# Contiguous head loads cast by DMA, head pairs in the halves of the PE array, and a sorting matrix spread by PE, in a block-sorted attention with an FFN behind it

## Chip, cores, metric

One core of a Trainium2 chip. The metric is device time in microseconds (us). "Span" is the time from the first to the last instruction in the trace; the timed run is about 2 us longer. A ratio is the mean time of one kernel's fast runs over the mean of the fast runs of the kernel before in the same rounds, so not quite the ratio of the medians that are quoted. Engines are PE (TensorE matmul), PEld (its weight loads), DVE (VectorE), ACT (ScalarE), POOL (GpSimd), SP (SyncE). "Granted clock" is the share of its full clock that PE was given; "eviction" is the copy of a product out of PSUM, where PE writes, into SBUF. In the lines of the profile scp are the scores, et their exponentials, vbp and vs the transposed v, oup the attention output, xtp its transpose, tp (before: ktp, vtp) the mixed k or v, qtp the transposed q, and hp and op the two products of the FFN.

## The reference, cut to what matters

```python
# q, k, v: (4 batches, 8 heads, 768 tokens, 64), sort_net: (4, 8, 8, 8); block = 96 tokens
P = sort_net
for _ in range(5):                       # exp, then divide by row sums and column sums
    ...
k_sorted = einsum('bhij,bhjcd->bhicd', P, k_blocks)     # mix the 8 blocks of k, and of v
v_sorted = ...
attn = softmax(scale * q_blocks @ k_sorted_blocks^T)    # 96 x 96 in each block
x = (attn @ v_sorted_blocks)  ->  (3072 tokens, 512)
out = relu(x @ w_in)**2 @ w_out                          # the FFN: 512 -> 2048 -> 512
```

There are 32 heads, which the changed kernel takes as 16 pairs, and 768 FFN matmuls of 128 x 128 by 512.

## The kernel before

What the change and the argument touch; `# ...` marks cuts.

```python
# sorting matrix: through DRAM, then spread to 128 partitions
nc.sync.dma_start(out=pt_dram.transpose([1, 0, 2]), in_=p_tr)
for j in range(NB):
    nc.sync.dma_start(out=ptall[16 * j:16 * j + 16, :, :],
                      in_=pt_dram[j].partition_broadcast(16))
w_all[...] = mask * ptall                      # DVE, per batch
# ...
for b in range(B):
    for h in range(H):                         # one head at a time
        # q as one load, k and v in 16-row pieces; q and k cast to bf16 on ACT
        for c in range(NC):
            nc.sync.dma_start(out=kf[:, c, :], in_=k_r[hd, :, 16 * c:16 * c + 16, :])
            nc.gpsimd.dma_start(out=vb[:, c, :], in_=v_r[hd, :, 16 * c:16 * c + 16, :])
        nc.scalar.copy(out=qb, in_=qf)
        nc.scalar.copy(out=kb, in_=kf)
        # ... transposes of q; k and v mixed by w_all; permuted on eviction
        for i in range(NB):
            nc.tensor.matmul(out=scp[:, i, 0:BLK], lhsT=ksT[:, i, :],
                             rhs=qT[:, BLK * i:BLK * (i + 1)], start=True, stop=True)
        nc.scalar.activation(out=et, in_=scp[:, :, 0:BLK], func=AF.Exp, scale=scale)
        # ... vs from vsT; then attn @ v with et as weights, divide, transpose to xT
for mc in range(MC):                           # FFN: matmuls, relu on ACT, square on DVE
    # ...
```

The softmax here doesn't subtract the row's maximum and nothing guards it: scores larger than these inputs give would overflow.

## Time and profile before

| | kernel before |
|---|---|
| median of 3 runs | 338.93 us (338.56 to 339.76) |
| span | 336.6 us |
| granted PE clock, mean | 0.954 |
| PE busy | 287.8 us (86%) |
| ACT busy | 130.2 us (39%) |
| exponentials | 32, 0.807 us each |

Two more lines of the page: the chain of waits that ended last, as shares of the span by engine, and the group of the exponentials (busy time, mean ns of one, idle time of ACT before them and what ended it).

```profile
PE 82%; SPq 6%; DVE 4%; DMA 4%; issue 1%; POOL 1%; ACT 1%; ACTq 0%; DVEq 0%
```

```profile
L198 ACT ACTIVATE et<-scp 96x768 bf16<-96x768 f32 x32 | 25.8, 807 | 38.6 <-PE scp L192 38.1
```

One exponential covers 768 columns in 807 ns.

### The profile page before, as it was taken

Reading aid. Unit: us, or ns where it says so; the run is one execution under the profiler, and the core shown is the slowest. Engines: PE = TensorE matmul, PEld = TensorE weight load, DVE = VectorE, ACT = ScalarE, POOL = GpSimd, SP = SyncE. Lnnn points to the kernel's source line nnn. Section 1 sums busy time; section 2 is a strip of 40 time slices with the busy share of each in tenths; the row PEclk is TensorE's granted clock in tenths of the full one; section 3 lists DMA queues with packets and bytes.
Section 4 is the critical chain, followed back from the end, with each engine's and each line's share of the span. In section 5 each row is a group of like instructions: output and inputs, shape, how many; then the busy total and the mean of one; then the engine's idle time right before and its main releaser. Section 6 shows DMA issues by size and latency. Waiting matters only on the chain.

```text
span 336.6 us, 6099 instructions
## 1 busy us (share of the span) xinstructions
PE 287.8 (86%) x2240; PEld 159.5 (47%) x2240; DVE 171.9 (51%) x338; ACT 130.2 (39%) x222; POOL 130.1 (39%) x267
## 2 busy tenths in 40 slices
PE   1012576776999999999999999999999999999995
PEld 0011455555555555555555555555544444444442
DVE  3443455655678655667765567776634204303400
ACT  3210322323455524365543255641136316425611
POOL 9483687447445564464455644650000000000000
PEclk9999995756799999999999999999999999999999
DMA  5579999857455575765556764321010010011011
GB/s 87 92 105 208 185 158 173 122 91 82 65 65 83 68 116 94 119 107 69 72 82 101 113 129 60 17 16 37 34 64 0 31 64 31 0 62 66 0 62 62
DMA packets 110366, 26.87 MB, mean 80 GB/s; under 512 B 104576, under 2 KB 106752, under 8 KB 110336
## 3 DMA queue, kind: packets, MB, share of 16 engines
q0 software_dynamic: 55104, 7.45, 26.2%
q1 hardware_dynamic: 55232, 19.03, 22.6%
q8 instruction: 17, 0.28, 0.3%
q14 instruction: 13, 0.11, 0.1%
HBM read 27.40 MB, written 6.30 MB: 100 GB/s over the span
## 4 chain that ended last, share of the span: by engine, by line
PE 82%; SPq 6%; DVE 4%; DMA 4%; issue 1%; POOL 1%; ACT 1%; ACTq 0%; DVEq 0%
PE hp L245 27%; PE op L257 26%; PE ktp L170 5%; PE oup L213 5%; PE vbp L203 5%; PE scp L192 4%; SPq L146 4%; PE qtp L161 4%; PE vtp L181 4%; DMA kf<-in_k_dram 4%; PE xtp L230 2%; DVE ao L222 2%; SPq L101 1%; DVE ksT L174 1%; DVE vs L208 1%
## 5 line engine op out<-in xcount | busy, mean ns | idle before, releaser
L150 POOL DMA_DIRECT2D vb<-in_v_dram x192 | 114.3, 626 | 85.6 <-PE vtp L181 76.1
L245 PE MATMUL hp<-xT,w_in_bf 128*128 128x512 bf16 x384 | 97.5, 385 | 0.0
L257 PE MATMUL op<-w_out_bf,h 128*128 128x512 bf16 x384 | 94.4, 380 | 0.0
L251 ACT ACTIVATE h<-hp 128x512 bf16<-128x512 f32 x96 | 57.2, 596 | 30.6 <-PE hp L245 30.5
L252 DVE TENSOR_TENSOR h<-h 128x512 bf16<-128x512 bf16 x96 | 40.0, 421 | 55.8 <-ACT h L251 55.5
L245 PEld LDWEIGHTS <-w_in_bf 128*128 128x128 bf16 x384 | 33.5, 98 | 36.2 <-issue 1.4
L257 PEld LDWEIGHTS <-h 128*128 128x128 bf16 x384 | 33.3, 98 | 35.6
L198 ACT ACTIVATE et<-scp 96x768 bf16<-96x768 f32 x32 | 25.8, 807 | 38.6 <-PE scp L192 38.1
L156 ACT CAST qb<-qf 128x384 bf16<-128x384 f32 x32 | 16.4, 512 | 52.4 <-PE qtp L161 50.4
L170 PE MATMUL ktp<-w_all,kb 128*64 128x128 bf16 x192 | 19.4, 247 | 19.3 <-DVE w_all L109 17.4
L174 DVE CAST ksT<-ktp 64x768 bf16<-64x768 f32 x32 | 30.3, 948 | 10.1 <-PE ktp L170 9.6
L263 ACT COPY ob<-op 128x512 f32<-128x512 f32 x24 | 14.0, 584 | 44.0 <-PE op L257 44.0
L185 DVE CAST vsT<-vtp 64x768 bf16<-64x768 f32 x32 | 30.1, 940 | 1.5 <-PE vtp L181 1.5
L157 ACT CAST kb<-kf 128x384 bf16<-128x384 f32 x32 | 16.4, 511 | 34.0 <-DMA kf<-in_k_dram 24.5
L208 DVE COPY vs<-vbp 96x512 bf16<-96x512 bf16 x32 | 13.5, 421 | 31.0 <-PE vbp L203 31.0
L170 PEld LDWEIGHTS <-kb 128*64 128x64 bf16 x192 | 14.3, 125 | 29.9 <-issue 21.6
L213 PE MATMUL oup<-vs,et 96*96 96x65 bf16 x256 | 18.1, 218 | 12.2 <-ACT et L198 7.7
L213 PEld LDWEIGHTS <-et 96*96 96x96 bf16 x256 | 15.3, 134 | 22.2 <-ACT et L198 13.0
L192 PEld LDWEIGHTS <-ksT 64*96 64x96 bf16 x256 | 15.2, 131 | 17.1 <-DVE ksT L174 12.8
L192 PE MATMUL scp<-qT,ksT 64*96 64x96 bf16 x256 | 19.3, 221 | 4.4 <-DVE ksT L174 4.4
L161 PE MATMUL qtp<-ident,qb 128*64 128x128 bf16 x192 | 18.7, 240 | 4.4 <-POOL mask L62 4.4
L222 DVE TENSOR_TENSOR ao<-oup,rec 96x512 bf16<-96x512 f32 x32 | 21.8, 683 | 0.7
(31 smaller groups left out, 168.3 us busy)
## 6 DMA issues: line engine op xcount, KB each, us to landing
qf<-in_q_dram SPq DMA_DIRECT2D x32, 192.0 KB
kf<-in_k_dram SPq DMA_DIRECT2D x192, 32.0 KB
out_dram<-ob SPq DMA_DIRECT2D x24, 256.0 KB
vb<-in_v_dram POOLq DMA_DIRECT2D x192, 16.0 KB, 2.3
w_in_bf<-in_moe_w_in_dram POOLq DMA_DIRECT2D x4, 512.0 KB, 8.7
w_out_bf<-in_moe_w_out_dram POOLq DMA_DIRECT2D x16, 128.0 KB, 4.8
ptall<-pt_scratch SPq DMA_DIRECT2D x8, 16.0 KB
p_sb<-in_sort_net_dram SPq DMA_DIRECT2D x1, 8.0 KB
```

Source lines behind the costliest of these rows:

```text
L150: nc.gpsimd.dma_start(out=vb[:, c, :], in_=v_r[hd, :, 16 * c:16 * c + 16, :],)
L161: nc.tensor.transpose(out=qtp[:, 128 * c:128 * (c + 1)], in_=qb[:, c, :], identity=ident)
L170: nc.tensor.matmul(out=ktp[:, 128 * c:128 * (c + 1)], lhsT=kb[:, c, :], rhs=wh, start=True, stop=True)
L174: nc.vector.tensor_copy(out=ksT.rearrange("p i (a c) -> p i a c", c=CH).transpose([0, 2, 1, 3]), in_=ktp.rearrange("p (a b c) -> p a b c", ...
L185: nc.vector.tensor_copy(out=vsT.rearrange("p i (a c) -> p i a c", c=CH).transpose([0, 2, 1, 3]), in_=vtp.rearrange("p (a b c) -> p a b c", ...
L192: nc.tensor.matmul(out=scp[:, i, 0:BLK], lhsT=ksT[:, i, :], rhs=qT[:, BLK * i:BLK * (i + 1)], start=True, stop=True)
L213: nc.tensor.matmul(out=oup[:, i, 0:D + 1], lhsT=et[:, i, :], rhs=vs[0:96, i, 0:D + 1], start=True, stop=True)
L222: nc.vector.tensor_tensor(out=ao2[:, :, h % 2, :], in0=oup[:, :, 0:D], in1=rec[:, :, None].to_broadcast([96, NB, D]), op=ALU.mult)
L245: nc.tensor.matmul(out=hp, lhsT=w_in_bf[:, kc, 128 * nt:128 * (nt + 1)], rhs=xT[:, kc, 512 * mc:512 * (mc + 1)], start=(kc == 0), stop=(kc ...
L251: nc.scalar.activation(out=h1, in_=hp, func=AF.Relu)
L252: nc.vector.tensor_tensor(out=h2[:, nt, :], in0=h1, in1=h1, op=ALU.mult)
L257: nc.tensor.matmul(out=op, lhsT=h2[:, nt, 128 * mt:128 * (mt + 1)], rhs=w_out_bf[:, nt, :], start=(nt == 0), stop=(nt == NT - 1))
```

## The change

Its intent: fewer and larger loads (a row is 6 tokens x 64 of one head, contiguous, and DMA casts), two heads at once in the halves of the PE array, full 128-column weights so that they load fast, and no trip through DRAM for the sorting matrix. Since a partition now holds the six consecutive tokens 6p to 6p+5, tokens come out of the products in another order: by a (0 to 5) first, then by c (0 to 15 in a block). They must be put back somewhere. For q nothing is done (the query order within a block is free until the output); for k and v the eviction reads PSUM permuted; for the exponential the write is permuted. The core of the diff:

```diff
-        kf, vb: 6 loads each per head (16 rows x 64); kb, qb cast by nc.scalar.copy
+    q_r = q.rearrange("b h (p a) d -> b p h (a d)", a=NA)          # NA = 6, likewise k, v
+    nc.gpsimd.dma_start(out=t[:, n * g:n * (g + 1), :], in_=src[b, :, n * g:n * (g + 1), :])
-    pt_dram store, eight broadcasts, w_all = mask * ptall
+    pt = ps1.tile([128, NB, NH], FP32, tag="p1")
+    for i in range(NB):
+        nc.tensor.matmul(out=pt[:, i, :], lhsT=pb[:, i, :, :]..., rhs=ident[0:NH, 0:NH], ...)
+    w_all = mask * pt
+    for a in range(NA):                       # q, k, v: both heads by turns, column halves
+        for e in range(2):
+            nc.tensor.matmul(out=tp[64 * e:64 * (e + 1), a, :], lhsT=src[:, hA + e, ...], rhs=w[e], ...)
+            nc.gpsimd.memset(sT[:, S:S + 32], 0.0)      # pads, behind the loads in GpSimd's queue
+        for hf in range(2):                   # scores: both heads by turns, row halves
+            scp = ps2.tile([128, 2, 512], FP32, tag="p2")
+            ...
-            nc.scalar.activation(out=et, in_=scp[:, :, 0:BLK], func=AF.Exp, scale=scale)
+            for e in range(2):
+                nc.scalar.activation(
+                    out=et[:, e, 384 * hf:384 * (hf + 1)].rearrange(
+                        "p (n c a) -> p n a c", c=C0, a=NA),
+                    in_=scp[0:96, e, 0:384].rearrange("p (n a c) -> p n a c", c=C0, a=NA),
+                    func=AF.Exp, scale=scale)
+                    # output: 128 columns of et as weights, 32 of them beyond the block
+                    lhsT=et[:, e, BLK * i:BLK * i + 128],
... FFN as before, but called between the pairs, with three PSUM buffers for both halves
```

## The prediction

> **What bounds the kernel now.** I read the 40 slices first, then a table of five stretches, then single stretches in order of time, then the waits.
>
> The slices split the run in three: PE is hardly busy up to slice 3, is patchy under a lowered clock in slices 5 to 10, and is full from there to the end.
>
> ```profile
> PE   1012576776999999999999999999999999999995
> PEclk9999995756799999999999999999999999999999
> ```
>
> The stretches, in us from the start of the span (columns: length; busy time and count of PE, PEld, DVE, ACT, POOL; granted clock; DMA share; GB/s):
>
> ```profile
> 0.00:37.00 37.00, 4.71 (x42) 4.06 (x42) 13.70 (x38) 7.12 (x15) 24.44 (x59) 1.00 0.80 126
> 37.00:86.00 49.00, 36.52 (x341) 28.54 (x341) 28.73 (x48) 12.81 (x21) 30.96 (x60) 0.71 0.91 130
> 86.00:110.00 24.00, 24.00 (x207) 12.82 (x204) 18.10 (x35) 14.43 (x25) 12.26 (x24) 0.94 0.53 73
> 144.00:250.00 106.00, 106.00 (x961) 57.98 (x960) 69.92 (x132) 46.11 (x79) 44.71 (x91) 1.00 0.46 69
> ```
>
> Start (0 to 37): 42 matmuls. Slow stage (37 to 86): about seven heads of attention, chains of dependent steps. Dense stage (86 to the end): PE never waits, so PE work is time. The chain of waits ends with pieces of 64 FFN matmuls in 13.81 us each, 0.2158 us per matmul; all 768 cost 165.7 us. In 144 to 250 lie 251 FFN matmuls (123 + 128): 54.2 us. The other 710 took 51.8 us, 0.073 each, so a head (46 of them) costs 3.36 us and a pair of heads 6.7.
>
> One group of eight score matmuls and six query transposes, early and late (timeline of PE; start, length):
>
> ```profile
> 53.39 0.87 PE L192 MATMUL scp<-qT,ksT 64*96 64x96 bf16 x8 [0.40 <-DVE ksT L174]
> 58.30 0.85 PE L161 MATMUL qtp<-ident,qb 128*64 128x128 bf16 x6
> 95.17 0.56 PE L192 MATMUL scp<-qT,ksT 64*96 64x96 bf16 x8
> 105.37 0.52 PE L161 MATMUL qtp<-ident,qb 128*64 128x128 bf16 x6
> ```
>
> The end of the last one is drawn long; by the distance from start to start, early groups run at 0.11 us per matmul (scp) and 0.12 to 0.13 (qtp), late ones at 0.06 and 0.077. So the slow stage is also a stage of half clock.
>
> The start is long because the sorting matrix goes through DRAM behind head loads and is then followed by a starved k load:
>
> ```profile
> DVE w_all L109 <- DMA ptall<-pt_scratch: 8.1, 1, 8.1
> ACT kb L157 <- DMA kf<-in_k_dram: 24.5, 6, 16.6
> ```
>
> The GpSimd timeline shows a thing that the change keeps: a DMA waits for an older one of its queue to land before it is even issued.
>
> ```profile
> 29.33 0.58 POOL L150 DMA_DIRECT2D vb<-in_v_dram  x1 [1.95 <-DMA w_in_bf<-in_moe_w_in_dram]
> 32.16 0.56 POOL L132 DMA_DIRECT2D w_out_bf<-in_moe_w_out_dram  x1 [2.25 <-DMA w_in_bf<-in_moe_w_in_dram]
> 34.73 0.54 POOL L132 DMA_DIRECT2D w_out_bf<-in_moe_w_out_dram  x1 [2.00 <-DMA w_in_bf<-in_moe_w_in_dram]
> ```
>
> The w_in pieces release them about 2.7 us apart; each reads 1.05 MB of float32, so a big casting load runs at about 385 GB/s of source.
>
> **What the Trainium skill says.** "TensorEngine Tiling (Array Packing)", Key Properties: different tiles can load weights and multiply in parallel, but changing the tiling mode drains the engine. The kernel before uses one half at a time, so the trace shows no such overlap; a lone FFN matmul between attention groups there spans about 0.3 us instead of 0.216, a cost of changing over. "TensorE: Matmul & The Clock Gate", Weight-path perf modes: fast weight load is on for 128 weights not in float32. The groups agree: 98 ns for 128 columns against 131 for 96 and 125 for 64. Same page, The HAM clock gate: PE runs at half clock until it has been busy for a window of some 3.4 us. That fits the halved rates above, and it doesn't say how dense is busy. "DMA: Bandwidth & Descriptors", Specifications: transfers under 512 B are read-modify-written. Queue 0 held 26.2% of 16 engines for 336.6 us, 1411 us; less about 350 us for 8.4 MB of weights, the 24576 v rows of 128 B cost 43 ns each, against 22 ns for a packet of queue 1, where nothing is cast (22.6%, 1217 us, 55232 packets).
>
> **The change, part by part.**
>
> *Loads.* Rows go from 256 B of source to 1536 B (768 B written), 12288 of them in place of 73728. My estimate is 75 ns a row (1536 B at the 24 GB/s per engine of w_in, and some overhead): batch 0 has 3072 rows, over 16 engines 14.4 us. The casts on ACT go (32.8 us), which were beside the path. In total DMA falls well under the span.
>
> *Sorting matrix.* An iteration took about 1.75 us undisturbed (11.56 to 13.29 is one). Five from 2.45 us end at 11.2; the spread product of 1024 elements about 1.2 us, eight matmuls at 0.11, and the first small w_all piece 0.4: the first k matmul at about 14 instead of 22.7. DVE builds the rest of w_all (0.95 + 3 x 1.22) before it touches vsT: about 18.7. Scores of pair 0 at 20.4.
>
> *A new wait.* In the built order of the changed kernel GpSimd issues all 22 loads (12 of batch 0, 4 of weights, 6 of batch 1) before the memsets of the pads of pair 0, and each DMA waits for the one eight before it. The last waits for the second half of w_in. Before that must land 4.7 MB at about 330 GB/s and 4.2 MB at 385: 14.4 + 10.9 + 3 of start = 28 to 29 us. The last two score matmuls and all of the attention output of pair 0 wait for that. So pair 1 starts at about 32, not 24.
>
> *Pairs 1 to 3 alone.* At half clock a pair has: 36 matmuls of q, k, v at about 0.1 (3.6), 8 xtp (0.8), three early FFN matmuls (1.3), 16 scores (1.3), eight vbp (1.0), vs copy and waits (1.1), output (0.7 for its first half), reciprocal and product (1.1): 10 to 11 us, at full clock about 8. Before, two heads took 13.4 (44.2 to 57.6). Three pairs at 9.7: the dense stage starts at 61 with eight heads done, instead of 86. Batch 1 has landed by about 55.
>
> *Dense stage.* A pair now has 84 matmuls in place of 92. q, k, v: 36 in alternating column halves, 0.077 before; I take 0.052, since two halves can overlap but a load and a matmul still issue for each: 1.87. Scores, 16 in row halves with fast weight load, 0.045: 0.72. vbp, eight at 0.072: 0.58. Output, 16 at 0.048: 0.77. xtp, eight at 0.054 as now: 0.43. Change-overs as now, 0.8: 6.7 for a pair, less 5.95, which 36 matmuls at 0.077, 16 scores at 0.062, 16 vbp at 0.06, 16 outputs at 0.05 and eight xtp at 0.054 make (late groups, from start to start). Sum 5.2. Twelve pairs 62; 756 FFN matmuls (12 are done early) 163. Small waits on eviction, since FFN work between steps is 16 to 20 matmuls a pair and PSUM has fewer buffers: 0.4 us a pair, 5. The tail after the last matmul stays 4.0 (332.6 to 336.6).
>
> DVE for a pair: vsT 0.94, qT 0.54, vs 0.7, two reciprocals 0.4, two products 1.36, xT 0.56: 4.5 us, 16 times 72, plus the FFN squares 40.0: well beside PE. ACT: one eviction 0.8 and four exponentials of 0.5, 45 us in all, plus 71 for the FFN. Neither binds.
>
> Sum: 61 + 62 + 163 + 5 + 4 = 295 of span. The time was 2.3 us over the span (338.9 against 336.6): 297. I shade to 295 since a faster clock in the slow stage seems likelier than a slower load.
>
> **The rivals.**
>
> *No overlap in the array.* Load and matmul of the other half don't run together. For it: q, k and v groups run at 0.077 though 128 columns of streaming at full rate take 0.054 (0.2158 x 128/512), so weight loads aren't hidden there. Against: their loads go to the same half. A pair then costs 6.3: 12 x 1.1 = 13 us more, 308. The gain is then nearly all of the start.
>
> *Full overlap and a warm early stage.* q, k, v at 0.04, scores at 0.03: 4.5 a pair, 8 us less; pairs 1 to 3 at 8 us each, 5 less; 282. For it: PE is denser in a pair than in a head. Against: 75% busy kept the clock at 0.71.
>
> *The load queue becomes the bound.* If casting rows of 1536 B run at 200 GB/s of source, the second half of w_in lands at 38, not 28, and batch 1 (15.5 MB in, to its first half) at about 67: 10 us more, 305. Against: w_in's 385.
>
> *Eviction latency becomes the bound.* One PSUM buffer for qtp, vbp and xtp, two for the rest, where in the dense stage one stalled step stops the FFN too, as PE runs in order: 1.5 us a pair would add 13, 308. Against: the FFN pieces between steps last 0.9 to 1.1 us, about a copy.
>
> **Range and chances.** Rivals one, three and four reach 305 to 308 alone, two together about 318; the good case is 282, with an early release of pair 0 some 276. Eight in ten: 276 to 312. To miss the 2% (332) would take nearly all rivals at once.
>
> **What would show it.** Right: first k matmul at 13 to 15; PE idle before the last scores of pair 0 until about 28, ended by a GpSimd memset; PE share over 95% from about 61; FFN alone still 13.81 us per 64; attention matmuls of 144 to 250 at about 0.062 each. Wrong: q, k, v groups still at 0.077 a matmul; a second wait for loads at the first k matmul of batch 1; scores or output waiting over 1 us in each dense pair.

## The result, and the profile after

| | before | after |
|---|---|---|
| median | 339.15 us (the runs beside it) | 349.88 us (349.08 to 350.28, 4 runs) |
| ratio | 1 | 1.03 (95%: 1.026 to 1.034) |
| span | 336.6 us | 348.0 us |
| granted PE clock, mean | 0.954 | 0.882 |
| PE busy | 287.8 us | 260.1 us |
| ACT busy | 130.2 us | 168.1 us |

The kernel became slower by 3%, where 295 us had been predicted. PE is busy 27.7 us less and ends later. (37 of the 2120 matmul records of the trace after, all of the FFN, are missing; the modelled ends of their neighbours cover most of them.) First the slices of the page after:

```profile
PE   0224566569669598766969999966867899999995
PEclk9999965688686899888689999988678899999999
```

The first part is what was hoped for: PE starts earlier. But the full block of nines that began at slice 10 (counted from 0) is gone: but for slices 21 to 25, PE is patchy up to slice 31, and its clock with it. The chain of waits after:

```profile
PE 62%; ACT 21%; issue 8%; DMA 6%; POOL 1%; DVE 1%; ACTq 0%; POOLq 0%
```

ACT went from 1% to 21% of the chain. The groups of the page say which of its instructions, and who waits for them:

```profile
L206 ACT ACTIVATE et<-scp 96x384 bf16<-96x384 f32 x64 | 85.0, 1595 | 20.9 <-PE scp L200 20.8
...
L231 PE MATMUL oup<-vs,et 96*128 96x65 bf16 x256 | 19.2, 220 | 51.7 <-ACT et L206 47.0
```

An exponential of **half** as many columns (384) is drawn with 1595 ns, **twice** as long as before, and PE sits idle 47.0 us in front of the output matmuls until one of them is done. One pair of the dense stage, in order of time (start, length, engine, line, what; in brackets the idle time before it and what ended it):

```profile
85.06 0.51 PE L200 MATMUL scp<-qT,sT 64*128 64x96 bf16 x16
85.45 5.28 ACT L206 ACTIVATE et<-scp 96x384 bf16<-96x384 f32 x4
85.51 0.62 PE L215 MATMUL vbp<-ident,sT 128*128 128x128 bf16 x8
85.97 1.03 PE L258 MATMUL hp<-xT,w_in_bf 128*128 128x512 bf16 x4
88.23 0.36 PE L231 MATMUL oup<-vs,et 96*128 96x65 bf16 x6 [1.24 <-ACT et L206]
89.51 0.20 PE L231 MATMUL oup<-vs,et 96*128 96x65 bf16 x1 [0.92 <-ACT et L206]
90.78 0.68 PE L231 MATMUL oup<-vs,et 96*128 96x65 bf16 x9 [1.07 <-ACT et L206]
...
93.84 0.85 PE L176 MATMUL tp<-w_all,kb 128*64 128x128 bf16 x12
...
98.37 0.51 PE L200 MATMUL scp<-qT,sT 64*128 64x96 bf16 x16
```

Three things are to be seen. The four exponentials take 5.28 us, 1.32 us each (the 1595 of the group counts their overlap twice). Behind the scores PE has eight transposes and four FFN matmuls, some 1.5 us, and then waits 3.2 us in three pieces. And the output matmuls come as 6, 1 and 9: the two heads go by turns, so six are the first three blocks, and numbers seven and eight are the fourth block. Its weights are read 128 columns wide from column 288, which reaches 32 columns into the second half of et. So seven waits for the third exponential and eight for the fourth, though the columns beyond 384 only make rows that nobody uses. After the waits PE is at half clock (0.50 granted from 89.8 to 96.6): the 12 matmuls of k take 0.79 us from start to start here (93.84 to the next thing at 94.63), against 0.45 in a pair at full clock (shown below). The pair takes 13.3 us from scores to scores, where the prediction had 5.2 of attention, 16 FFN matmuls (3.45) and 0.4 of waits: 9.05.

### The profile page after: what moved, and what is told of

It is laid out like the page before. It is cut to its first block, busy times and chain, and to the rows that moved or that the text cites. A ratio compares the mean times of both kernels' runs of the same rounds, so it can differ in the third digit from the quotient of the medians.

```text
span 348.0 us, 5090 instructions
## 1 busy us (share of the span) xinstructions
PE 260.1 (75%) x2083; PEld 138.1 (40%) x2120; DVE 119.8 (34%) x260; ACT 168.1 (48%) x206; POOL 31.9 (9%) x104
## 4 chain that ended last, share of the span: by engine, by line
PE 62%; ACT 21%; issue 8%; DMA 6%; POOL 1%; DVE 1%; ACTq 0%; POOLq 0%
PE op L270 24%; PE hp L258 23%; ACT et L206 17%; PE tp L176 6%; DMA w_in_bf<-in_moe_w_in_dram 4%; PE xtp L247 3%; PE qtp L162 2%; ACT h L264 2%; PE oup L231 2%; DMA kb<-in_k_dram 2%; DVE ao L239 1%; PE scp L200 1%; ACT sT L185 0%; POOL qb L72 0%; POOL vb L72 0%
## 5 line engine op out<-in xcount | busy, mean ns | idle before, releaser
L206 ACT ACTIVATE et<-scp 96x384 bf16<-96x384 f32 x64 | 85.0, 1595 | 20.9 <-PE scp L200 20.8
L270 PE MATMUL op<-w_out_bf,h 128*128 128x512 bf16 x375 | 85.1, 382 | 0.6 <-issue 0.2
L231 PE MATMUL oup<-vs,et 96*128 96x65 bf16 x256 | 19.2, 220 | 51.7 <-ACT et L206 47.0
L231 PEld LDWEIGHTS <-et 96*128 96x128 bf16 x256 | 13.3, 113 | 61.9 <-ACT et L206 55.9
L185 ACT CAST sT<-tp 128x768 bf16<-128x768 f32 x16 | 12.8, 799 | 27.8 <-PE tp L176 27.8
L247 PE MATMUL xtp<-ident,ao 96*128 96x96 bf16 x128 | 15.8, 270 | 2.7 <-DVE ao L239 2.3
L247 PEld LDWEIGHTS <-ao 96*128 96x128 bf16 x128 | 12.2, 132 | 13.3 <-issue 8.1
L220 DVE COPY vs<-vbp 96x1024 bf16<-96x1024 bf16 x16 | 11.0, 686 | 18.6 <-PE vbp L215 18.6
L187 DVE CAST sT<-tp 128x768 bf16<-128x768 f32 x16 | 15.3, 957 | 3.7 <-PE tp L176 3.7
L200 PE MATMUL scp<-qT,sT 64*128 64x96 bf16 x256 | 9.7, 217 | 9.0 <-POOL sT L188 8.0
```

Source lines behind the costliest of these rows:

```text
L187: nc.vector.tensor_copy(out=view, in_=tpv)
L200: nc.tensor.matmul(out=scp[:, e, BLK * n:BLK * (n + 1)], lhsT=ksT[64 * e:64 * (e + 1), BLK * i:BLK * i + 128], rhs=qT[64 * e:64 * (e + 1), ...
L206: nc.scalar.activation(out=et[:, e, 384 * hf:384 * (hf + 1)].rearrange("p (n c a) -> p n a c", c=C0, a=NA), in_=scp[0:96, e, 0:384].rearra ...
L231: nc.tensor.matmul(out=oup[:, e, 66 * n:66 * n + D + 1], lhsT=et[:, e, BLK * i:BLK * i + 128], rhs=vs[:, i, e, 0:D + 1], start=True, stop= ...
L247: nc.tensor.transpose(out=xtp[:, i, :], in_=ao[:, i, :, :].rearrange("p e d -> p (e d)"), identity=ident[0:96, 0:96])
L270: nc.tensor.matmul(out=op, lhsT=h2[:, nt, 128 * mt:128 * (mt + 1)], rhs=w_out_bf[:, nt, :], start=(nt == 0), stop=(nt == NT - 1))
```

## The experiments

Theory: the exponential is dear because of its scattered write; PE's wait for it and the half clock that follows are the whole loss. Rivals: the smaller number of columns or the PSUM read makes it dear; the pads behind the loads cost the time; the halves of the array don't overlap. Times are medians.

### The write of the exponential alone

> The changed kernel with one edit: the permutation inside the exponential is done on the side that reads PSUM, so that et is written contiguously. Theory A (the 12-byte step of the bf16 writes makes each exponential take 1.32 us instead of about 0.5, and PE waits for it in every pair): exponentials at about 0.5 us, a dense pair falls from 13.3 us to about 8.5, time about 284 us, between 276 and 296. Rival B (few PSUM buffers and eviction latency hold the pairs, the exponential is only the last of the waits): exponentials at 0.5 us but a dense pair still above 11 us, time above 315 us. Rival C (it is the walk in runs of 16, whichever side has it, that is slow): exponentials stay above 1 us, time about 345 us.

```diff
-                    out=et[...].rearrange("p (n c a) -> p n a c", c=C0, a=NA),
-                    in_=scp[0:96, e, 0:384].rearrange("p (n a c) -> p n a c", c=C0, a=NA),
+                    out=et[...].rearrange("p (n c a) -> p n c a", c=C0, a=NA),
+                    in_=scp[0:96, e, 0:384].rearrange("p (n a c) -> p n c a", c=C0, a=NA),
```

The same values go to the same places; only the walk differs: read with a step, write flat. **272.33 us** (270.16 to 273.69), ratio 0.802 (0.797 to 0.806), clock 0.987. PE's and DVE's instructions stand in the same order as in the changed kernel. The page and one pair in order of time:

```profile
PE 230.2 (85%) x2083; PEld 122.9 (45%) x2120; DVE 117.9 (44%) x260; ACT 110.3 (41%) x206; POOL 31.9 (12%) x104
...
L206 ACT ACTIVATE et<-scp 96x384 bf16<-96x384 f32 x64 | 26.3, 489 | 22.9 <-PE scp L200 22.9
```

```profile
66.99 0.51 PE L200 MATMUL scp<-qT,sT 64*128 64x96 bf16 x16
67.38 1.62 ACT L206 ACTIVATE et<-scp 96x384 bf16<-96x384 f32 x4
67.89 1.03 PE L258 MATMUL hp<-xT,w_in_bf 128*128 128x512 bf16 x4
69.00 0.67 PE L231 MATMUL oup<-vs,et 96*128 96x65 bf16 x16
74.25 0.52 PE L200 MATMUL scp<-qT,sT 64*128 64x96 bf16 x16
```

Four exponentials take 1.62 us, the output follows without a wait as one group of 16, and a pair takes 7.26 us instead of 13.3. The span falls by 77.2 us. It splits in two: PE's idle time falls by 47.3 (348.0 - 260.1 against 270.8 - 230.2), nearly all of it the 47.0 of waits for the exponentials, and PE's busy time for the same matmuls by 29.9, which fits the lower clock (busy time times mean granted clock is 229 before and 227 now; both traces lack the same number of records).

> The kernel before with one edit, wrong result on purpose: its exponential of 768 elements writes with the 12-byte step inside each block. Theory A: 2.5 us instead of 0.807 each, 32 of them are 54 us more of ScalarE; the dense stage of this kernel has slack on ScalarE, so only part reaches the time: 345 to 375 us instead of 339. Rival C predicts the same duration, rival B (scattering is harmless) leaves it at 0.8 us and 339 us.

The other way round: the kernel **before** with the scattered write and all else as it was.

```diff
-                out=et, in_=scp[:, :, 0:BLK], func=AF.Exp, scale=scale)
+                out=et.rearrange("p i (c a) -> p i a c", a=6),
+                in_=scp[:, :, 0:BLK].rearrange("p i (a c) -> p i a c", a=6), ...)
```

This permutes queries within a block, which is wrong; scores are so small here that softmax is nearly even (worked out from the reference's inputs, every weight lies within about 2% of 1/96). So the check says nothing on the order of the queries within a block, and the permutation in the good versions was checked by reading. **383.97 us**, ratio 1.132 (1.125 to 1.139): the direction of the theory, but more than the 345 to 375 that it expected.

```profile
L198 ACT ACTIVATE et<-scp 96x768 bf16<-96x768 f32 x32 | 87.1, 2722 | 38.5 <-PE scp L192 37.9
```

The 768 columns went from 807 to 2722 ns (2.5 us expected), and PE now waits for ACT in front of its output here too (49.6 us in 31 waits; 7.7 in one before). The cost belongs to the write and not to the rest of the change.

### What the write costs, measured by itself

> The kernel of e1 with ten kinds of 384-element instructions added at the end, three of each, to measure the disputed cost by itself; PSUM is the source of all. Theory A: ScalarE flat about 0.5 us, step of 6 bf16 about 1.3 us, read with a step and flat write about 0.5 us. Open, and measured here: a step of 2 bf16, runs of two bf16 (4 bytes) with a step, float32 with a step of 6, Copy instead of Exp, and VectorE flat against step 6. If the loss comes from writes narrower than some unit, runs of two and float32 are cheaper than single bf16; if it comes from the step alone they are as slow.

> The kernel of e1 with single-level exponentials of 384 elements from PSUM added at the end, three of each: bf16 written with a step of 1, 2, 3, 4, 6, 8, 16 elements, float32 with a step of 1, 2, 3, 4, 8. Known so far: bf16 step 1 0.49 us, step 2 0.59, the kernel's step of 6 in runs of 16 1.44; float32 in that walk 0.86. If the cost goes with the distance in bytes, it grows from 4 to 12 bytes and then levels off, and float32 with a step of 12 bytes is as slow as bf16 with 12; if it is the 2-byte width with a gap, float32 stays under 0.9 at every step and bf16 is slow from step 3 on.

> The changed kernel with the flat exponential and, three times each, single exponentials of 96 x 384 from PSUM written in seven patterns. The earlier steps fit 186 ns plus 4.3 ns for every stretch of 16 bytes that the write enters (bf16), or 1.7 ns (float32). Theory (stretches entered count, no matter how far apart): step of 4 single bf16: 1016 as before; two single elements 8 bytes apart in every other stretch (192 entries): 1010 to 1030; the packed row written by turns in two neighbouring stretches (384 entries): 1850 or so; four neighbours in each stretch (96 entries): about 600; pairs of neighbours, one pair a stretch (192 entries): 1010; eight neighbours in every other stretch (48 entries): 500 to 510; float32 by turns in two stretches (384 entries): 840. Rival (the distance to the next element up to 16 bytes counts, 0.27 ns a byte): the second pattern about 1440, the pairs about 1060 to 1200. Rival (an element that has a neighbour before it in order is merged with it): pairs well under 1010, near the 724 of the pairs measured before, and the alternating row dear.

All three add probe instructions behind the end of a full kernel; their times (287.68, 300.39 and 284.18 us, one run each) mean nothing else. Each probe writes 96 x 384 values from PSUM, three times. From the first (flat; the kernel's walk; the same walk on the read side; the kernel's walk by VectorE):

```profile
L318 ACT ACTIVATE pr_act_flat<-prs 96x384 bf16<-96x384 f32 x3 | 1.5, 487 | 5.0 <-DVE pr_dve_f32step L331 5.0
L320 ACT ACTIVATE pr_act_step<-prs 96x384 bf16<-96x384 f32 x3 | 4.3, 1438 | 0.0
L325 ACT ACTIVATE pr_act_readstep<-prs 96x384 bf16<-96x384 f32 x3 | 1.7, 552 | 0.0
L330 DVE CAST pr_dve_step<-prs 96x384 bf16<-96x384 f32 x3 | 4.3, 1420 | 0.0
```

The scattered write costs three times the flat one; the scattered PSUM read costs 65 ns. VectorE pays the same (1420 against 554 flat), and a plain copy on ScalarE 1449, so it is neither the function nor the engine, but the write. The second probe, by the step between single values:

| step of the write, bf16 | 1 | 2 | 3 | 4 | 6 | 8 | 16 |
|---|---|---|---|---|---|---|---|
| ns for 384 | 512 | 593 | 807 | 1016 | 1438 | 1862 | 1767 |
| stretches of 16 bytes entered | 48 | 96 | 144 | 192 | 288 | 384 | 384 |

The Trainium skill has a place that would have warned me, and the prediction did not use it: "Advanced Engine Details and Errata", Memory Cachelines, says that SBUF is kept in lines of 16 bytes, that following accesses to one line run at full speed, and that each access to a different line pays a penalty. The third row above counts these lines. From step 2 to step 8 the times fit 180 ns plus 4.36 ns for each line entered within about 1%: 96 lines give 599 (593 measured), 192 give 1017 (1016), 288 give 1436 (1438), 384 give 1854 (1862). Steps 1 and 16 lie outside this fit: the flat row takes 512 for its values alone, and step 16 (1767) is 5% below it. Float32 at steps of 2, 3, 4 and 8 (504, 671, 839, 852 ns) gives 1.7 ns a line over the same 180; at step 1 it read 683 ns, which fits nothing and stays unexplained. This was fitted after the fact, so the third probe tested it against two rivals, that the distance to the next value counts, and that a value is merged with a neighbour written just before it:

| pattern of 384 values | lines entered | ns |
|---|---|---|
| single bf16, 8 bytes apart (as above) | 192 | 1035 |
| two single bf16, 8 bytes apart, in every other line | 192 | 971 |
| a packed bf16 row, written by turns in two neighbouring lines | 384 | 1868 |
| pairs of bf16 neighbours, one pair a line | 192 | 503 |
| four bf16 neighbours a line | 96 | 487 |
| eight bf16 neighbours, every other line | 48 | 487 |
| float32 row, by turns in two lines | 384 | 837 |

The second row ends the rival that counts the distance to the next value (about 1440 expected). The third shows that a **packed** target is as dear as a scattered one, if the order of writing changes the line every time. The fourth is against my own count of lines, which said 1010: a pair of neighbours, one pair a line, costs no more than the flat row (487 to 512). This and the dear third row are what the second rival had expected. So what is dear is a lone two-byte value in a new line, 4.3 ns; a float32 in a new line costs 1.7. For pairs the runs give no one figure: in the first probe 192 pairs written 128 bytes apart took 724 ns. Why two bytes cost more than four no run shows.

### The pads behind the loads

> The changed kernel, slow exponential kept, with the pads and the ones written once by VectorE into two fixed copies of the tiles ahead of the loads, so that no GpSimd memset waits behind the queue of loads. If the start's wait was worth its 8 us: the last scores of pair 0 at about 20 us instead of 28.6, all later steps 8 us earlier, time about 342 us. If the wait only hides another one (the data of batch 1, or w_in for the first FFN matmuls): time 346 to 350 us.

```diff
+    for j in range(2):                       # two fixed copies of ksT, vsT, et, vs
+        nc.vector.memset(sTs[n][j][:, S:S + 32], 0.0)   # and et's pads, vs's ones: before the loads
-            nc.gpsimd.memset(sT[:, S:S + 32], 0.0)      # and the other two, in each pair
```

The scattered exponential stays. **341.03 us**, ratio 1.005 (1.001 to 1.009): 8.9 us less than the changed kernel. In order of time, PE's scores of the first pair, first of the changed kernel, then of this one:

```profile
28.57 0.26 PE L200 MATMUL scp<-qT,sT 64*128 64x96 bf16 x2 [7.99 <-POOL sT L188]
```

```profile
19.20 0.83 PE L209 MATMUL scp<-qT,ksT 64*128 64x96 bf16 x16 [0.65 <-DVE qT L178]
```

The wait that the prediction saw in the built order is real (8.0 us until 28.57), and worth about its length, but it was in the predicted 295 already. It isn't the miss.

> Both edits together: the permutation on the read side of the exponential, and pads and ones written once ahead of the loads. The start's wait was worth 9 us in the slow kernel (349.9 to 341.0). If it is as free of others here: time about 264 us. If batch 1 or the weights then come too late for the first dense pair: 267 to 272 us.

Both corrections together: **264.19 us** (263.26 to 265.59), ratio **0.777** (0.774 to 0.780), right result. This is the best version and beats both kernels. PE's slices of it:

```profile
PE   0047778899999999999999999999999999999993
```

PE is full from about 50 us to the end and busy 89% of the span.

### The halves of the array, and the sorting matrix

> The kernel of e1 with the same matmuls of q, k, v and scores in another order: all of one head, then all of the other, so that neighbours in the queue use the same half of the array. Theory (alternating halves overlap, as the step on the PE array in the prediction says): groups of twelve q, k or v matmuls go from about 0.46 us to about 0.92 (0.077 each, as in the kernel before), scores from 0.45 to 0.6 or more; about 1.3 us a pair, 12 dense pairs and more, time 285 to 292 us instead of 272. Rival (the halves bring nothing by themselves, the gain comes from other things, such as fewer and larger groups): the groups keep their length, time 270 to 275 us.

```diff
-        for a in range(NA):
-            for e in range(2):
+        for e in range(2):                   # q, k, v and scores: one head, then the other
+            for a in range(NA):
```

On the version with the flat exponential: **274.95 us**, ratio 0.809 against 0.802 with the heads by turns. PE in order of time, without the turns, then (from the run with the read side) with them:

```profile
103.88 0.66 PE L176 MATMUL tp<-w_all,kb 128*64 128x128 bf16 x12
104.47 0.39 PE L258 MATMUL hp<-xT,w_in_bf 128*128 128x512 bf16 x1
```

```profile
70.88 0.53 PE L176 MATMUL tp<-w_all,kb 128*64 128x128 bf16 x12
71.33 0.39 PE L258 MATMUL hp<-xT,w_in_bf 128*128 128x512 bf16 x1
```

The time falls in the rival's range (270 to 275, from "the halves bring nothing by themselves"), but that isn't what it shows. From start to start a group of 12 takes 0.59 us without turns and 0.45 with, where a group of six took 0.455 in the kernel before. The timeline merges a group; the single records in the trace show what lies behind this (medians of the groups after 110 us):

| group of 128-column matmuls, dense stage | first start to last start | last start to the FFN matmul behind it |
|---|---|---|
| 6 of one head, kernel before | 0.303 us | 0.152 us |
| 12 of two heads by turns | 0.307 us | 0.152 us |
| 12 of two heads, one after the other | 0.445 us | 0.152 us |

With turns, two heads take the time of one: their matmuls start in pairs, 3 to 4 ns apart, and a pair follows the other by 0.052 to 0.056 us, as single matmuls did before. Without turns twelve would span some 0.64 us if nothing overlapped (an estimate: 0.303 and six more at 0.056); they span 0.445, since the second head's matmuls start between those of the first all the same (one at 104.011, the other's at 104.017). So this edit leaves more than half of the overlap in place, and what it costs is the worth of the order, not of the halves: a dense pair takes 7.69 us instead of 7.26. In the total this shows only in part, as the early pairs came 6.8 to 7.3 us apart in this run's trace, against 7.1 to 8.2 with the turns, where the clock fell twice before 52 us. The scores are a clearer case: without turns they still start in pairs, 13 to 14 ns apart, and 16 take 0.46 us against 0.45. No run here takes the overlap away altogether.

> The kernel before with one part of the change alone: the sorting matrix spread over partitions by PE instead of by a trip through DRAM. The first k matmul comes at about 15 us instead of 22.7. Theory (in the kernel before the start is held by the k load that is starved behind v and weights loads, not by the matrix): time 335 to 340 us, under 2% gained. Rival (the matrix is what holds the start): time 331 us or less.

The kernel before with only the sorting matrix spread by PE: **333.46 us**, ratio 0.980 (0.978 to 0.982), between what theory and rival expected. The first k matmul starts at 17.84 us instead of 22.66, but the first output still waits (6.92 us, until 30.75) for the exponential, whose place in ACT's queue is behind the cast of a late k load. Worth 2%: a real gain, but a small one, since its interval includes 2%.

### How long may the exponential be?

If only its length matters, a flat exponential made as long must cost the same.

> The kernel of e1, each flat exponential executed twice into the same place (same result): the four of a pair take about 3.2 us of ScalarE instead of 1.6. Theory (only the time that ScalarE needs between scores and output matters, not how it writes): the FFN work behind vbp covers little of it, a dense pair grows from 7.3 us to about 9, time between 290 and 305 us. Rival (scattered writes hurt beyond ScalarE's own time, for instance other engines' access to SBUF): under 280 us, since twice a short exponential is still mostly hidden.

> The same three times: about 4.9 us of ScalarE in a pair, against the 5.3 us of the changed kernel. Theory: a dense pair at 12 to 13 us with the clock lowered in the waits, time 325 to 348 us, near the 349.9 of the changed kernel. Rival (the writes themselves disturb other engines): well below that, under 310 us.

```diff
-            for e in range(2):
+            for e in [0] * 3 + [1] * 3:      # the same exponential three times (or twice)
```

**281.62 us** twice, **296.89 us** thrice (ratio 0.871). Both missed what I had expected (290 to 305, and 325 to 348), and the second fell where the rival had put it (under 310: the scattered write disturbs more than its own length): the 12 flat exponentials take 4.80 us a pair, nearly the 5.28 of the four scattered ones, and the kernel is 53 us faster than the changed one. The trace of PE shows why that wasn't a fair comparison:

```profile
104.11 4.80 ACT L206 ACTIVATE et<-scp 96x384 bf16<-96x384 f32 x12
104.62 3.19 PE L270 MATMUL op<-w_out_bf,h 128*128 128x512 bf16 x14
108.06 0.40 PE L231 MATMUL oup<-vs,et 96*128 96x65 bf16 x7 [0.26 <-ACT et L206]
```

PE's order is laid when the kernel is built. With twelve exponentials in the program it put 12 to 14 FFN matmuls between the scores and the output; for four, whatever their walk, it puts 4. The second factor is therefore this: **the order was laid for a short exponential, and PE runs it in order.** The next runs pin the order by hand (FFN matmuls handed out one by one inside the pair).

> Control. The changed kernel with its slow exponential, PE's order pinned by hand to what it was in the dense stage: 1, 1, 5, 4, 5 FFN matmuls after k, v, q, vbp and output of a pair (four early FFN groups of three are left out, q follows v). Both theories: a dense pair about 13 us, ScalarE's exponentials 1.32 us, time 345 to 358 us.

> The same with 12 FFN matmuls between vbp and the output, 2 more in its middle and 28 instead of 16 a pair, as in the order that the build gave to the kernel with three executions of the exponential. Theory (two causes multiply: the exponential takes 5.3 us of ScalarE a pair, and the order in PE's queue was laid for one of 1.6, so PE stands in front of the output while FFN work that is ready lies behind it): PE's waits for the exponential in a dense pair fall from about 3.3 us to about 1, time 300 to 320 us, with the exponentials still at 1.32 us. Rival (the scattered write itself slows the rest, whatever the order): 335 us or more.

```diff
+        fill(4)      # e11: as built before      ->  fill(12)   # e12: FFN matmuls before the output
```

Both with the scattered exponential: **359.51 us** with the built order rebuilt by hand (ratio 1.056; just above its expected range, so the hand order costs some 10 us), **331.98 us** with 12 matmuls in front of the output and 28 instead of 16 in a pair (ratio 0.974), between theory and rival. The order, with the FFN matmuls that it moves into the pairs, is worth 27.5 us, but 35 us to the 297 of the flat ones were open. PE in order of time in this second run:

```profile
88.01 2.54 PE L261 MATMUL hp<-xT,w_in_bf 128*128 128x512 bf16 x11
90.39 0.35 PE L233 MATMUL oup<-vs,et 96*128 96x65 bf16 x6
91.56 0.20 PE L233 MATMUL oup<-vs,et 96*128 96x65 bf16 x1 [0.82 <-ACT et L207]
92.84 0.20 PE L233 MATMUL oup<-vs,et 96*128 96x65 bf16 x1 [1.07 <-ACT et L207]
```

The first group runs at once, and then the fourth block waits for the third and fourth exponential: the overlap of its 128-wide weights. Taking the halves in reverse order removes it, because blocks 4 to 7 reach only into the pads, and blocks 0 to 3 come last anyway.

> The kernel with the scattered exponential and the fitting order of PE (332 us), with the two halves of a pair's blocks taken in the reverse order (blocks 4 to 7 first) and 8 FFN matmuls between the two output groups. The trace of it before shows the output as 6 matmuls, a wait of 0.8, one, a wait of 1.07, one more: the weights of the fourth block are read 128 columns wide and reach 32 columns into the next half, so the last two matmuls of the first output group wait for the third and fourth exponential. Reversed, the first group reads only its own half and the pads. Theory (what is left in the 332 is this overlap, and the half clock that its waits bring): the two waits fall into FFN work, some 2 us and 1 to 2 us of half clock in each of 12 pairs: 295 to 310, granted clock over 0.96. Rival (relus queued behind the exponentials with three PSUM buffers, or the scattered write itself, hold it): 320 or more.

```diff
-        for hf in range(2):
+        for hf in (1, 0):                    # scores and exponentials, and the output
-            fill(2 if hf == 0 else 6)
+            fill(8 if hf == 1 else 4)
```

**314.68 us**, ratio 0.925 (0.920 to 0.930), clock 0.987: 17.3 us less, still with the scattered write. The edit does two things at once, since it also puts 8 and 4 FFN matmuls behind the two output groups in place of 2 and 6, 32 a pair instead of 28; no run takes them apart. A pair of the first half of an FFN piece and a pair of the second half, in order of time:

```profile
95.69 0.42 PE L233 MATMUL oup<-vs,et 96*128 96x65 bf16 x8
98.57 1.89 PE L261 MATMUL hp<-xT,w_in_bf 128*128 128x512 bf16 x8 [2.45 <-ACT h L269]
...
109.55 0.42 PE L233 MATMUL oup<-vs,et 96*128 96x65 bf16 x8
109.81 1.89 PE L276 MATMUL op<-w_out_bf,h 128*128 128x512 bf16 x8
```

The output runs as a whole group of eight, and in the second case nothing waits: that pair takes 11.0 us. In the first the FFN now waits 2.45 us for a relu, which stands behind the four exponentials in ACT's queue while the three PSUM buffers are full. The profile adds up 14.7 us of this wait; less these, the kernel would be at about 300 us (an estimate from these two numbers), which is in the range expected for the theory. So it lies between theory (295 to 310) and rival (320 or more), and the relus that the rival had named make up the difference.

> The same pinned order of PE as the 332 us kernel, halves not reversed, with the exponential written flat and done three times (4.8 us a pair in place of 5.28). Theory (the scattered write costs its duration alone): 0.5 us less a pair, a little over that with the half clock: 315 to 330. Rival (the scattered write disturbs PE or VectorE beside its duration): under 310, near the 297 of the flat exponential done thrice in the scheduler's own order.

The pinned order of the 332 us run with three flat exponentials in place of each scattered one: **314.40 us**, ratio 0.927, just below the range for "it costs its length alone" (315 to 330) and above the rival's (under 310). The two flat kernels differ by 17.5 us (296.89 and 314.40), so half of the 35 us belongs to the pinned order; 17.6 are left between the scattered and the flat write in the same order. The waits of PE for them are about as long in both (29.2 and 31.0 us in all). The difference lies mostly in PE's busy time (241.2 against 255.5 us), and that in the clock: 0.988 against 0.941. VectorE was not disturbed (busy 120.5 us in both). The granted clock changes in steps of 3.41 us: the 11 falls of the 332 us run follow steps in which PE was busy for 38 to 51%; this run has two falls, both after 49%, and keeps the full clock after other steps of 49 to 58%. So a slightly shorter exponential (4.80 against 5.28) goes with a PE just busy enough to keep its clock, and some of the damage is a step and not in proportion. This was read afterwards, and no run tests it.

### A second way to the right order

> The changed kernel with the permutation moved one step up: VectorE writes qT in token order from a PSUM read with a step, so that the scores come out in token order and the exponential is flat on both sides. Theory: exponentials about 0.41 us in a row as in e1; the qT copy no longer reads neighbours and grows from 0.55 to 0.95 us, beside PE; time 270 to 277 us, the same as e1 within 2%. If VectorE's copy lands on the path of every pair: up to 285 us.

```diff
-        qT = att.tile([128, NB, NA, C0], ...)     # out=qT, in_=qtp "p i a c"
+        qT = att.tile([128, NB, C0, NA], ...)     # out=qT, in_=qtp "p i c a": q in token order
-                    (exponential permuted)
+                    out=et[:, e, 384 * hf:384 * (hf + 1)], in_=scp[0:96, e, 0:384],
```

Here VectorE's copy of q does the reordering on its read and the exponential is flat on both sides: **271.69 us**, ratio 0.798 (0.795 to 0.801), the same as with the permuted read (0.802) within the intervals. The copy of q grew from 0.55 to 0.95 us, as expected, and costs nothing to be seen.

## Why the prediction was wrong

- **The failed step**, as the prediction put it: "*ACT: one eviction 0.8 and four exponentials of 0.5, 45 us in all, plus 71 for the FFN. Neither binds.*" The eviction is 0.8 as said. An exponential is 1.32 us in a row, 5.28 for four. I took 0.5 from 807 ns for 768 columns, and did not look at the walk of the output. ACT stays far from busy (48%), and still binds: PE has 1.5 us of work while it waits for the four, and gets the last after 5.3. "Not busy" had been read as "not in the way".
- **The rival "eviction latency becomes the bound"** was the right kind of wait, at the wrong step and too small: 1.5 us a pair, 308, with the FFN pieces between steps set against "about a copy". The sum itself had "*0.4 us a pair, 5*" for small waits. With the true length of the exponential the waits are 3.2 us in the pair shown (47.0 in all), and the lower clock adds 29.9 to PE's busy time; the prediction had no term for a clock that falls again in the dense stage. 271 of span with the flat write, plus 47.3, plus 29.9, is 348.
- **What was not seen**: the fourth block's weights reach into the next half, so the first output group waits for all four exponentials (17.3 us at the fitting order, with the FFN matmuls moved in the same edit), and the built order has only four FFN matmuls in front of the output.
- **Start: right.** First k matmul at 13.1 (about 14 predicted), the pads' wait ends at 28.6 (28 to 29), worth 8.9 us.
- **Early pairs**: 11.5 us apart against 10 to 11; with the flat write 7.1 to 8.2.
- **PE's work in a pair: too dear.** With the flat write the pair takes 7.26 us, of which 16 FFN matmuls are 3.45: 3.8 for the attention against the predicted 5.2. Terms: q, k, v 0.038 a matmul against 0.052, scores 0.028 against 0.045, vbp 0.056 against 0.072, output 0.032 against 0.048. With the flat write, the rival "full overlap" would have been the right one, with its 282 even beaten (272.3). So a second error, of the other sign, hid in the 295: had only the exponential been as short as assumed, 295 would have been too much by 23.
- **"No overlap in the array"** and **the load queue as the bound** are refuted: twelve matmuls of two heads span 0.307 us where six of one spanned 0.303, and with the pads first PE never waits for a load. The argument for the first was a misreading: 0.077 spreads the change-over to the next group (0.152 us) over six matmuls, and within a group they start 0.056 us apart, close to the 0.054 of streaming, so the loads were hidden already.
- **The clock.** The prediction quoted a window of some 3.4 us for the half rate. The trace of the dense pair shows half clock with no gap of PE longer than 1.24 us. The granted clock changes in steps of 3.41 us, and the falls go with the sum of the waits within a step: PE was busy for 1.20 of the 3.41 us from 86.36 to 89.77, and at half clock for the 6.8 us from there. All 15 falls of the changed kernel follow steps with 17 to 41% busy, and no step with 62% or more is followed by one. That is no threshold for every kernel: the kernel before falls after 63 to 70%, and the run with the halves reversed keeps its clock after 41%. (The clock records begin with the first rise, at 38.6 us here. Before it the profile shows full clock, but the q transposes at 17.5 us start 0.107 us apart per pair of heads, where they later start 0.053 apart; so all mean clocks in this text are too high by that start.) The Trainium skill's page "TensorE: Matmul & The Clock Gate" has, besides the window, a section "A second HAM failure mode: psum-queue depth-cycling", which tells of a kernel where frequent short idles between groups let the clock go back and forth. The clock here does the same; the idles come from waits for ACT.

## What to carry to other kernels

Ask of each layout change on which side the permutation lands: read it permuted and write it flat, and look at the order in which bytes of the output follow each other, not at how many there are. An engine that is busy less than half the time (48% here) binds as soon as its result takes longer (5.3 us) than the work that the waiting engine has queued before it (1.5 us), and that queue was laid when the kernel was built, with the same four FFN matmuls for the scattered and the flat write. Check also what an over-wide operand reads beyond its block: it can be a dependency that no arithmetic needs.

## What the Trainium skill lacked or had wrong

- "Advanced Engine Details and Errata", Memory Cachelines: right that lines of 16 bytes matter, without a cost. The runs give one for writes: 4.3 ns for every line that lone bf16 values enter, 1.7 ns for float32. It asks for at least two hits on a line to hide the latency; two are not enough here: a step of 4 bf16, two hits a line, took 1016 ns against 512 flat, while two neighbouring values, one pair a line, were free (503).
- "SBUF — State Buffer", Door 1: The DMA port swizzle, says that one can step for free over up to 8 bf16 values. Not for writes: a step of 2 took 593, of 3 807, of 6 1438, of 8 1862 ns.
- "ScalarE: Activation LUTs", What ACT_TABLE_LOAD costs: 186 ns and 0.833 ns a value, for every function, would be 506 ns for 384 values (an estimate from the page's figures); measured 487 to 512 flat, 552 with a permuted PSUM read, and 1438 with the kernel's write. The page doesn't say that the write's pattern can triple it. VectorE's copy went from 554 to 1420 ns in the same way.
- "TensorE: Matmul & The Clock Gate", The HAM clock gate: gives "no PE-idle gaps >~3.4µs" as the rule. That is not enough: here the longest gap of the dense stage is 1.95 us, three gaps of 0.9 to 1.25 us in a pair of 13.3 us were enough, and the clock was 0.83 on average from 60 to 200 us. It gives no number for how busy PE has to be within a window.
- No page gives the cost of a change-over between groups of small matmuls: in the dense stage 0.152 us pass between the last start of a group of 128-column matmuls and the FFN matmul behind it, against 0.056 within the group.
